# Attention outputs weighed after the products, and three of its operands turned by VectorE and DMA in place of TensorE

## The chip, the cores and the metric

The kernel runs on one core of a Trainium2 chip. A core has TensorE (PE in the profile, its weight loads PEld), VectorE (DVE), ScalarE (ACT), GpSimd (POOL) and SyncE (SP), which here only issues transfers (its issues stand as SPq). Each engine works through its own queue in order. TensorE writes to PSUM, the other engines read and write SBUF, and DMA moves data between SBUF and DRAM. The metric is the device time of one execution in microseconds (us). Before the change it is 2302.33 us, the median of 3 runs (2301.53 to 2303.08).

## The reference

The input is x, 2048 tokens of 1024 features, in float32. What is computed, cut to what matters:

```python
x = A_x
h  = x + A(layernorm(x), wq, wk, wv, wo, beta)   # Infini-attention
h2 = h + B(layernorm(h), w1, b1, w2, b2)         # layernorm, MLP 1024 -> 3584 -> 1024 with gelu

# A: 32 heads of 32 features, 4 segments of 512 tokens, one after the other
for s in range(4):
    logits = qs @ ks.T * Dh**-0.5 + mask         # per head, within the segment; causal
    a_dot  = softmax(logits) @ vs
    a_mem  = (phi(qs) @ M) / (phi(qs) @ z + 1e-6)   # phi(t) = t + 1 where t > 0, else exp(t)
    outs.append(g * a_mem + (1 - g) * a_dot)     # g = sigmoid(beta), one per head
    M += phi(ks).T @ vs                          # a 32x32 memory per head
    z += phi(ks).sum()                           # over the segment's tokens
A = concat(outs) @ wo
```

## The kernel before, in words

All products are made in float32r from two parts, a high part (the value rounded) and a low part (what is left), as three matmuls: high by high, high by low, low by high.

The program works in two halves of 1024 tokens, that is two segments each. A half has its attention first, then the product with wo, then the MLP's first layer; the MLP's second layer follows once, at the end, for all tokens.

The attention of a half is 16 **units**: 8 groups `g` of four heads, and for each the half's two segments. With segments numbered `s` = 0 to 3, the first half holds s = 0 and 1, the second s = 2 and 3, so each s has 8 units, and there are 32 in all. Queries, keys and values come out of the projections with features in the partitions (4 heads of 32) and 512 tokens along the row.

`dense` (L402) does a unit's projections: 8 steps each for keys, queries and values (`project`, L355; three matmuls of 512 columns a step). Around them it makes high and low parts (kh, kl, qh, ql) and `stack` (L372) puts these together for each head by DMA: a unit has 24 such transfers of 64 KB, all issued by SP on line 377. It also makes phi of keys (pk) and queries (pq). Three operands must be turned, so that tokens and features change places, and TensorE does it by matmuls with an identity, four of 128x128 each time:

- phi(keys), where s < 3: L453 into `pkn` in PSUM; ACT takes the high part (pkh, L455), DVE the low (pkl, L457),
- values, in every unit: ACT copies them to SBUF (vt, L461), TensorE turns them (vn, L469), ACT and DVE make the two parts of vs (L471, L472),
- what was read from the memory, where s > 0: `om` is turned on L516 into `pom`, and ACT copies that to `omt` (L521).

The memory's own small products (pm, pmm) wait in a list, and `one_small` (L383) puts one of them before a transpose or a product of the softmax part.

The softmax part of a unit runs while the next unit is projected: `heads` yields steps (L631), and `interleave` takes one for each step of `dense`. A **slot** is one head, and the string `PLAN` (L31) says what each of a slot's six steps does: `q` products of queries and keys, then mask, maximum and exponential with sums (`qk`, `soft`); `n` the weighing (`norm`, L552: DVE inverts the sums two blocks at a time, and POOL multiplies the exponentials, `pr`, by the inverse and by 1 - g, L557); `t` transposes of the weighed blocks (`ptr`, L560) with a copy to the high part; `s` the low part; `a` the products with vs (`av`, L582); `o` the output (`av_out`, L600). Three heads are under way at once: the current one (q, n), the one before (t, s) and the one before that (a, o). After a unit's fourth head POOL adds omt to the output tile ot (L607), and ot goes to DRAM.

The order on each engine is made when the program is built: the instructions are placed in the order of the program where what they need is there in time by the builder's own estimate, and a later one may be put first. PSUM has three banks for projections and turned operands (`ps_dense`); SBUF has five tiles of name `tmp`, six of `tmpr`, one `ot`.

Of the kernel before, what the change touches and what calls it, by code (L numbers as in the profile page):

```python
# [17 lines left out]
P = 128  # L18
# [12 lines left out]
PLAN = ('q1 S2', 'q0 n0 a0', 'q2 t0 a1', 'q3 n2 s0 o', 't1', 's1 t2')  # L31
# [8 lines left out]
def raw(ap):  # L40
    return ap.bitcast(F32)


def build(tc, x, wq, wk, wv, wo, beta, w1, b1, w2, b2, out):
# [8 lines left out]

    ident = const.tile([P, P], F32, name="ident")
# [29 lines left out]

    acts = {}
# [258 lines left out]
    def attention(half, first):  # L344
# [6 lines left out]

        def tmpr(name):
            return ab.tile([P, 512], F32R, tag="tmpr", name=name, bufs=6)
# [48 lines left out]
        def dense(g, sl, ws, u):  # L402
            s = 2 * half + sl
            behind = acts.pop("late", iter(()))
            kps = ws.pop("kps", None)
            if kps is None:
                kps = ps_dense("kps")
                for c in project(ws["k"], sl, "kps", kps):
                    if c >= 2:
                        next(behind, None)  # L410
                    yield
            kh, kl = tmpr("kh"), tmpr("kl")
            nc.scalar.copy(kh, kps)
            nc.vector.tensor_tensor(kl, kps, raw(kh), op=ALU.subtract)
            if s < 3:
                kparts = phi_parts(kps)
            qps = ps_dense("qps")
            for c in project(ws["q"], sl, "qps", qps):
                if c == 0:
                    u["ks"] = stack(kh, kl, "ks", (0, 1, 0))  # L420
                if c == 2 and s < 3:
                    zc = ab.tile([P, 64], F32, name="zc", bufs=2)[:, 0:1]
                    pk = phi_sum(kparts, "pk", zc)
                next(behind, None)
                yield
            qh, ql = tmpr("qh"), tmpr("ql")
            nc.scalar.copy(qh, qps)
            nc.vector.tensor_tensor(ql, qps, raw(qh), op=ALU.subtract)
            if s > 0:
                qparts = phi_parts(qps)  # L430

            vps = ps_dense("vps")
            for c in project(ws["v"], sl, "vps", vps):
                if c == 0:
                    u["qs"] = stack(qh, ql, "qs", (0, 0, 1))
                if s > 0:
                    if c == 2:
                        pq = phi_sum(qparts, "pq")
                    if c == 4:
                        while small:  # L440
                            one_small()
                        pqh, pql = tmpr("pqh"), tmpr("pql")
                        mzh = ab.tile([P, 256], F32R, name="mzh", bufs=1)[:, 0:132]
                        mzl = ab.tile([P, 256], F32R, name="mzl", bufs=1)[:, 0:132]
                        nc.scalar.copy(pqh, pq)
                        nc.gpsimd.tensor_copy(mzh, MZ[:, g, :])
                        nc.gpsimd.tensor_tensor(mzl, MZ[:, g, :], raw(mzh), op=ALU.subtract)
                    if c == 5:
                        nc.gpsimd.tensor_tensor(pql, pq, raw(pqh), op=ALU.subtract)
                if c == 1 and s < 3:  # L450
                    pkn = ps_dense("pkn")
                    for i in range(4):
                        nc.tensor.transpose(pkn[:, i * P:(i + 1) * P], pk[:, i * P:(i + 1) * P], ident)  # L453
                    pkh, pkl = tmpr("pkh"), tmpr("pkl")
                    nc.scalar.copy(pkh, pkn)  # L455
                if c == 2 and s < 3:
                    nc.vector.tensor_tensor(pkl, pkn, raw(pkh), op=ALU.subtract)  # L457
# [986 lines left out]
```

## Time and profile before

| | |
|---|---|
| time, median of 3 runs | 2302.33 us (2301.53 to 2303.08) |
| span of the profiled execution | 2296.2 us |
| busy: PE, PEld | 2270.4 us (99%), 1890.8 us (82%) |
| busy: DVE, ACT, POOL | 1540.3 us (67%), 1225.0 us (53%), 1092.4 us (48%) |
| attention of the first half, of the second | from the start to about 500 us; from about 900 to 1400 us |

The span reaches from the first instruction's start to the last one's end; the run's time holds it and what lies around it. A row of a group of instructions reads: line, engine, operation, out<-in, shapes, count, then busy time, mean ns of one, and the idle time of the engine before them with what ended it. Matmuls overlap in the pipeline, so a row's duration of one matmul is longer than the distance to the next one's start; the chain of waits counts by such distances.

### The profile page before, as it was taken

To read this page: it belongs to the slowest core of one execution; us is meant where nothing else is said; L and a number is where in the kernel's file an instruction comes from. 1 tells how busy PE (TensorE), PEld (TensorE's weight loads), DVE (VectorE), ACT (ScalarE), POOL (GpSimd) and SP (SyncE) were. 2 spreads that over 40 slices of the span, in tenths; PEclk is the share of its full clock that TensorE was granted. 3 is DMA by queue.
4 is the path that set the end of the run, shared out by engine and by line. 5 is a ranking of instruction groups with operands and counts; after the bars stand their busy time and mean duration, and the time that the engine had idled before them with its cause. 6 is when DMAs were issued, how large, how long until landed. Compare 5 with 4: busy or idle time off the path is not lost.

```text
span 2296.2 us, 35279 instructions
## 1 busy us (share of the span) xinstructions
PE 2270.4 (99%) x11769; PEld 1890.8 (82%) x11769; DVE 1540.3 (67%) x3173; ACT 1225.0 (53%) x2549; POOL 1092.4 (48%) x1134
## 2 busy tenths in 40 slices
PE   8999999999999999999999999999999999999999
PEld 6888888878888888888888887888888888888887
DVE  6777777776655565777777777565566766577563
ACT  6777777775453445777777776363344223322221
POOL 5545555555244442555555556253445554155430
PEclk9999999999999999999999999999999999999999
DMA  6333333345465654433333344466667976476762
GB/s 190 92 85 91 93 89 85 87 120 182 139 204 172 188 165 142 113 91 86 85 87 88 87 111 140 156 211 175 176 188 263 345 243 216 159 253 221 249 234 90
DMA packets 322719, 355.36 MB, mean 155 GB/s; under 512 B 26190, under 2 KB 218730, under 8 KB 322538
## 3 DMA queue, kind: packets, MB, share of 16 engines
q1 hardware_dynamic: 259370, 316.40, 45.4%
q10 hardware_dynamic: 63168, 36.71, 5.3%
q8 instruction: 93, 1.52, 0.3%
q14 instruction: 88, 0.72, 0.1%
HBM read 226.59 MB, written 76.09 MB: 132 GB/s over the span
## 4 chain that ended last, share of the span: by engine, by line
PE 91%; ACT 3%; POOL 2%; DVE 2%; issue 1%; DMA 1%; ACTq 0%; SPq 0%; POOLq 0%; DVEq 0%
PE po L1278 22%; PE bps L882 9%; PE cps L882 7%; PE dps L882 6%; PE po L593 6%; PE ppt L573 6%; PE pqk L541 3%; PE vps L116 2%; PE vps L115 2%; PE kps L115 2%; PE kps L116 2%; PE vps L117 2%; PE kps L117 2%; PE pwo L117 2%; PE pwo L116 2%; PE pwo L115 2%
## 5 line engine op out<-in xcount | busy, mean ns | idle before, releaser
L557 POOL TENSOR_SCALAR pr<-pr,nm,gate 128x128 f32<-128x128 f32 (+3 forms) x512 | 322.6, 639 | 345.9 <-DVE nm L554 260.0
L550 ACT ACTIVATE pr<-pr,mx 128x256 f32<-128x256 f32 (+3 forms) x512 | 287.6, 562 | 161.9 <-DVE mx L542 158.2
L580 DVE TENSOR_TENSOR ptl<-ppt,pth 128x512 fp32r<-128x512 f32 (+1 forms) x384 | 227.2, 599 | 86.2 <-ACT pth L575 82.0
L542 DVE CUSTOM_DVE_ANT_0 pr<-pqk,mask 128x256 f32<-128x256 f32 (+3 forms) x512 | 243.3, 484 | 46.5 <-PE pqk L541 43.7
L573 PE MATMUL ppt<-ident,pr 128*128 128x128 f32 x1280 | 223.6, 277 | 2.1 <-POOL pr L557 1.4
L575 ACT CAST pth<-ppt 128x512 fp32r<-128x512 f32 (+1 forms) x384 | 194.2, 517 | 39.0 <-PE ppt L573 33.1
L1288 DVE TENSOR_TENSOR c<-c,po 128x512 f32<-128x512 f32 x160 | 105.4, 683 | 143.1 <-PE po L1278 135.5
L573 PEld LDWEIGHTS ppt<-ident,pr 128*128 128x128 f32 x1280 | 164.6, 140 | 32.5 <-POOL pr L557 2.6
L541 PE MATMUL pqk<-ks,qs 96*128 96x256 f32 (+3 forms) x512 | 161.3, 315 | 0.0
L92 POOL TENSOR_TENSOR wl<-wr,wh 128x1024 fp32r<-128x1024 f32 x52 | 124.5, 2393 | 70.8 <-PE pqk L541 27.6
L593 PE MATMUL po<-pth,vs 128*64 128x512 f32 (+3 forms) x512 | 155.4, 326 | 0.3 <-ACT pth L575 0.2
L593 PE MATMUL po<-ptl,vs 128*64 128x512 f32 (+3 forms) x512 | 153.9, 310 | 1.3 <-DVE ptl L580 1.2
L1278 PE MATMUL po<-w2h,zh 128*128 128x512 f32 x378 | 121.1, 390 | 0.8 <-DVE zh L1218 0.4
L1135 POOL TENSOR_TENSOR w2r<-w2r 128x512 f32<-128x512 f32 x54 | 85.4, 1593 | 72.0 <-DVE c L1288 36.9
L541 PEld LDWEIGHTS pqk<-ks,qs 96*128 96x128 f32 x512 | 96.2, 188 | 21.5
L994 POOL TENSOR_TENSOR s<-r 128x512 f32<-128x512 f32 x28 | 43.6, 1559 | 143.4 <-DVE sa L1010 87.1
L882 PE MATMUL bps<-zh,sb 128*128 128x512 f32 x336 | 111.0, 391 | 0.0
L882 PE MATMUL bps<-zh,sa 128*128 128x512 f32 x336 | 110.8, 390 | 0.0
L115 PE MATMUL vps<-yh,wh 128*128 128x512 f32 x256 | 109.4, 427 | 0.9 <-DVE MZ L497 0.9
L115 PE MATMUL kps<-yh,wh 128*128 128x512 f32 (+1 forms) x264 | 110.1, 417 | 0.0
L115 PE MATMUL qps<-yh,wh 128*128 128x512 f32 x256 | 106.8, 417 | 0.0
L1278 PE MATMUL po<-w2h,hl 128*128 128x512 f32 x322 | 103.2, 390 | 0.5 <-POOL hl L1218 0.3
(241 smaller groups left out, 6657.1 us busy)
## 6 DMA issues: line engine op xcount, KB each, us to landing
hr<-h_dram SPq DMA_DIRECT2D x112, 448.0 KB, 5.4
w2r<-in_B_w SPq DMA_DIRECT2D x122, 256.0 KB, 4.4
r<-in_B_w SPq DMA_DIRECT2D x56, 512.0 KB, 4.5
h_dram<-ht ACTq DMA_DIRECT2D x84, 256.0 KB, 3.7
ks<-kh SPq DMA_DIRECT2D x256, 64.0 KB, 2.0
qs<-qh SPq DMA_DIRECT2D x256, 64.0 KB, 2.0
wr<-in_A_wo SPq DMA_DIRECT2D x32, 512.0 KB, 4.0
wx<-in_B_w SPq DMA_DIRECT2D x56, 256.0 KB, 3.5
```

Source lines behind the costliest of these rows:

```text
L115: nc.tensor.matmul(ps, ah, bh, start=first, stop=False)
L116: nc.tensor.matmul(ps, ah, bl, start=False, stop=False)
L541: nc.tensor.matmul(pqk[:, :n], u["qs"][j][:, i * P:(i + 1) * P], u["ks"][j][:, 0:n], start=True, stop=True)
L542: nc.vector.tensor_tensor_reduce(out=st["pr"][:, offs[i]:offs[i] + n], in0=pqk[:, :n], in1=mask[:, 512 - n:512], op0=ALU.add, op1=ALU.min, ...
L550: nc.scalar.activation(pi, pi, AF.Exp, bias=mx[:, i:i + 1], scale=-1.0, accum_out=mx[:, 4 + i:5 + i])
L557: nc.gpsimd.tensor_scalar(pi, pi, nm[:, 4 + k:5 + k], gate[:, 1, 4 * g + j:4 * g + j + 1], op0=ALU.mult, op1=ALU.mult)
L573: nc.tensor.transpose(ppt[:, o:o + P], pr[:, offs[i] + jk * P:offs[i] + (jk + 1) * P], ident)
L575: acts["pth"] = n, nc.scalar.copy(pth[:, base:base + w], ppt[:, :w])
L580: nc.vector.tensor_tensor(o, x0, x1, op=ALU.subtract)
L593: nc.tensor.matmul(po[:, P * jk:], v, st[part][:, koff[jk]:koff[jk] + w], start=(jk, part) == (0, "pth"), stop=(jk, part) == (2, "ptl"))
L882: nc.tensor.matmul(ps, x_[:, c, :], y_[:, c, :], start=first and c == 0 and n == 0, stop=last and c == 3 and n == 2, skip_group_check=True)
L1278: nc.tensor.matmul(ps, x_[:, k], y_[k], start=opens and k == 0 and i == 0, stop=closes and k == self.KP - 1 and i == 2, skip_group_check=True)
```

## The change

Three things change in the attention; the MLP and the product with wo stay.

1. *The weighing.* `norm` goes: the exponentials are turned and multiplied with vs as they are. `inverse` (`r` in PLAN) makes the inverse of a head's four sums, and, at the fourth head, multiplies them by 1 - g on POOL. `weigh` (`w`), once in a unit, turns these 16 columns by one TensorE transpose, copies them to SBUF, stores them in DRAM and loads them back spread over the partitions, as a tile w of 128x512. `av_out` multiplies the unit's output by w on POOL.
2. *The turning.* `turned` takes the place of the TensorE transposes of values, phi(keys) and om: DVE transposes within 32x32 blocks, SP stores the result in DRAM (256 KB) and loads it back in four transfers of 32 partitions, which puts the blocks in their places. The tiles for it are taken from the pool of the half (`zt`), whose tiles wo_first uses afterwards. The heads' and blocks' order in vs changes with it, and POOL makes pkl.
3. *The order.* `dense` becomes a table: `TIMES` gives each part a step, 0 to 23 in the unit's own projections, 24 and more in the next unit's. PLAN is new as well. The parts for `VT`, `KT` or `OT` being False are not used.

```diff
-PLAN = ('q1 S2', 'q0 n0 a0', 'q2 t0 a1', 'q3 n2 s0 o', 't1', 's1 t2')
+VT, KT, OT = True, True, True
+TIMES = dict(pk=10, kx=15, pkh=21, pkl=22, ks=12, qs=16, pq=17, pqh=19, pql=20, omt=20, vx=23, pm=25, vs=32, vl=33, pmm=38, om=37, omc=40)
+PLAN = ('r', 'q0', 'a0 S2 t0 q2 s0', 'a1 q1 o', 't1 s1 w q3', 't2')
...
+    PKL, VSL, GTE = nc.gpsimd, nc.vector, nc.gpsimd
...
+    turn_dram = [dram.tile([P, 512], F32, name=f"turn_dram{k}") for k in range(6)]
+    r_dram = [dram.tile([16, P], F32, name=f"r_dram{k}") for k in range(2)]
...
+        scr = [acts["zt"].tile([P, 4, 512], F32, tag=f"t{x_}3", name=f"sc{x_}") for x_ in "hl"]
+
+        def turned(src, to, mid):
+
+            nc.vector.transpose(mid.rearrange("p (c k d) -> p c k d", c=4, k=4), src.rearrange("p (k c d) -> p c k d", c=4, k=4))
+            d = turn_dram[acts.get("turned", 0) % len(turn_dram)]
+            acts["turned"] = acts.get("turned", 0) + 1
+            nc.sync.dma_start(d, mid)
+            for c in range(4):
+                nc.sync.dma_start(to[32 * c:32 * c + 32].rearrange("j (h x) -> j h x", h=4),
+                                  d[:, c * P:(c + 1) * P].rearrange("(h j) x -> j h x", h=4))
...
+            def on(name, fn):
+                t = T[name]
+                (todo if t < 24 else after).setdefault(t % 24, []).append(fn)
...
+            def key_turn():
+                v["kn"] = scr[1][:, 2 + sl]
+                turned(v["pk"], v["kn"], scr[1][:, 0])
+
+            def key_halves():
+                v["pkh"], v["pkl"] = tmpr("pkh"), tmpr("pkl")
+                v["pkn"] = v["kn"].rearrange("p (h k d) -> p k h d", h=4, k=4)
+                v["pk4"] = [x_.rearrange("p (k h d) -> p k h d", h=4, k=4) for x_ in (v["pkh"], v["pkl"])]
+                nc.scalar.copy(v["pk4"][0], v["pkn"])
+
+            def key_lower():
+                PKL.tensor_tensor(v["pk4"][1], v["pkn"], raw(v["pk4"][0]), op=ALU.subtract)
...
+            def value_turn():
+                v["vn"] = scr[0][:, 2 + sl]
+                turned(ps["v"], v["vn"], scr[0][:, 0])
...
+            def value_halves():
+                v["vn3"] = v["vn"].rearrange("p (h k e) -> p h k e", h=4, k=4)
+                nc.scalar.copy(vs.rearrange("p (h k) e -> p h k e", h=4)[:, :, :, 0:32], v["vn3"])
+
+            def value_lower():
+                v4 = vs.rearrange("p (h k) e -> p h k e", h=4)
+                VSL.tensor_tensor(v4[:, :, :, 32:64], v["vn3"], raw(v4[:, :, :, 0:32]), op=ALU.subtract)
...
+            def memory_turn():
+                while v.get("read") != 1:
+                    one_small()
+                turned(v["om"], u["omt"], tmp("omx"))
...
-        def norm(st, i):
-            pr, mx, nm, j, g = st["pr"], st["mx"], st["nm"], st["j"], st["u"]["g"]
-            nc.vector.reciprocal(nm[:, 4 + i:6 + i], mx[:, 4 + i:6 + i])
-            for k in (i, i + 1):
-                pi = pr[:, offs[k]:offs[k] + P * (k + 1)]
-                nc.gpsimd.tensor_scalar(pi, pi, nm[:, 4 + k:5 + k], gate[:, 1, 4 * g + j:4 * g + j + 1],
-                                        op0=ALU.mult, op1=ALU.mult)
+        def inverse(st):
+            u, j = st["u"], st["j"]
+            if j == 0:
+                u["rs"] = ab.tile([P, P], F32, name="rs", bufs=1)
+            rs = u["rs"]
+            nc.vector.reciprocal(rs[:, 4 * j:4 * j + 4], st["mx"][:, 4:8])
+            if j == 3:
+                r4 = rs[:, 0:16].rearrange("p (h i) -> p h i", i=4)
+                GTE.tensor_tensor(r4, r4, gate[:, 1, 4 * u["g"]:4 * u["g"] + 4].unsqueeze(2).to_broadcast([P, 4, 4]),
+                                        op=ALU.mult)
+
+        def weigh(st):
+            u, j = st["u"], st["j"]
+            if j < 3:
+                return
+            n = acts["weighed"] = 1 - acts.get("weighed", 0)
+            w = u["w"] = tmp("w") if u["g"] == NG - 1 and u["s"] % 2 else scr[n][:, 1]
+            pw = ps_dense("pw")
+            nc.tensor.transpose(pw[0:16, 0:P], u["rs"][:, 0:16], ident)
+            nc.scalar.copy(w[0:16, 0:P], pw[0:16, 0:P])
+            d = r_dram[n]
+            nc.sync.dma_start(d, w[0:16, 0:P])
+            nc.sync.dma_start(w, bass.AP(tensor=d.tensor, offset=d.offset, ap=[[512, 4], [0, DH], [1, 512]]))
...
-                v = u["vs"][:, 4 * jk + j, :]
+                v = u["vs"][:, 4 * j + jk, :]
...
             if j == 3:
+                nc.gpsimd.tensor_tensor(ot, ot, u["w"], op=ALU.mult)
                 if u["omt"] is not None:
-                    nc.gpsimd.tensor_tensor(ot, ot, u["omt"], op=ALU.add)
+                    if OT:
+                        ot4 = ot.rearrange("p (k c j) -> p k c j", k=4, c=4)
+                        nc.gpsimd.tensor_tensor(ot4, ot4, u["omt"].rearrange("p (c k j) -> p k c j", k=4, c=4), op=ALU.add)
```

More of the change, by code (lines that the diff above doesn't have):

```diff
@@ L427, in dense @@
[L427 to L435, printed above, removed]
-                if s > 0:
[L437 to L457, printed above, removed]
-                next(behind, None)
-                yield
@@ L530, in attention @@
+            run(24)
+            acts["carry"] = after
         offs = [0, 128, 384, 768]
```

245 lines of the change are left out of this document (153 added, 92 removed).

## The prediction

> **What bounds the kernel now.** I read the page's busy line and chain first, then the windows of the two attention stretches, since nothing else is changed.
>
> ```profile
> span 2296.2 us, 35279 instructions
> PE 2270.4 (99%) x11769; PEld 1890.8 (82%) x11769; DVE 1540.3 (67%) x3173; ACT 1225.0 (53%) x2549; POOL 1092.4 (48%) x1134
> PE 91%; ACT 3%; POOL 2%; DVE 2%; issue 1%; DMA 1%; ACTq 0%; SPq 0%; POOLq 0%; DVEq 0%
> ```
> ```profile
> 100.00:300.00 200.00, 199.60 (x1220) 169.31 (x1219) 148.50 (x437) 145.45 (x370) 105.38 (x148) 1.00 0.33 83
> 1000.00:1200.00 200.00, 200.00 (x1225) 169.69 (x1224) 151.59 (x452) 146.81 (x373) 112.51 (x150) 1.00 0.35 88
> ```
>
> A window's row gives its length, then PE, PEld, DVE, ACT and POOL busy, the granted clock (1.00), the DMA engines' busy share and GB/s. In both stretches PE is busy all the time, DVE three quarters, ACT nearly as much, POOL a half, the DMA engines a third. A busy PE could still hide waits, so I looked at who makes PE wait, in the waits, and at the chain through a middle stretch (its row: start, us, what).
>
> ```profile
> PEld po L593 <- DVE ptl L580: 8.5, 19, 0.7
> PEld pmm L395 <- ACT r L364: 2.1, 7, 0.3
> PE ppt L573 <- POOL pr L557: 1.4, 4, 0.5
> POOL pr L557 <- DVE nm L554: 260.0, 120, 9.8
> ```
> ```profile
> 181.88 0.44 PE pkn L453 x4
> 192.63 0.44 PE vn L469 x4
> 199.05 0.59 ACT kh L413
> ...
> 260.94 0.59 ACT kh L413
> ```
>
> POOL's weighing makes PE wait 1.4 us in all; its own 260 us are waits of an engine that nobody waits for. So PE's stream of matmuls is the bound in the attention, and its time there is the sum of the distances between its starts. The copies of keys to kh are one per unit; two units lie between 199.05 and 260.94 (a third copy between them is not on the chain), which makes 30.95 us a unit and, at 24 steps, 1.29 us a step.
>
> **Part 1: what leaves TensorE.** The rows of the three turned tiles give the counts.
>
> ```profile
> L469 PE MATMUL vn<-ident,vt x128: 271/272/329, 40.6 to 1380.8; 128*128 128x128 f32 x128
> L453 PE MATMUL pkn<-ident,pk x96: 270/272/273, 31.5 to 1333.3; 128*128 128x128 f32 x96
> L516 PE MATMUL pom<-ident,om x96: 270/296/331, 80.5 to 1387.9; 128*128 128x128 f32 x96
> ```
>
> These are 128 + 96 + 96 = 320 transposes, 80 groups of four. Which price: the duration of one is 272 ns, but the chain puts a group of four at 0.44 us, 110 ns each, what it takes to start the next work. For pkn and vn that row is the very thing. The four of pom have small products between them:
>
> ```profile
> 204.26 0.22 PE L395 MATMUL pmm<-vs,pkl 128*128 128x128 f32 x1
> 204.32 0.27 PE L516 MATMUL pom<-ident,om 128*128 128x128 f32 x1
> 204.35 0.31 PE L395 MATMUL pmm<-vs,pkh 128*128 128x128 f32 x1
> 204.50 0.30 PE L516 MATMUL pom<-ident,om 128*128 128x128 f32 x1
> ```
>
> From small product to transpose 0.06 us, then 0.03, then 0.15: a pair takes 0.18 to 0.19, so a transpose adds up to 0.13 us, a group 0.5 us. But the small products are not removed; they go between other transposes or products and pay part of it there. I take 0.44 for all: 80 x 0.44 = 35.2 us, upper end 38. The unknown is only whether the time stays gone.
>
> [...]
>
> **Part 2: what comes to TensorE.** `weigh` makes one transpose in each of 32 units. A quarter of a group is 0.11 us, and alone it is no more than a group's 0.44: 3.5 to 14 us. I take 3.5, since the group's 0.44 is nearly even per transpose.
>
> **Part 3: the other engines, which must not become late.**
>
> ```profile
> L472 DVE TENSOR_TENSOR vs<-vn,vs 128x512 fp32r<-128x512 f32 x32 | 22.0, 686 | 0.7 <-ACT vs L471 0.4 <-DMA qs<-qh 0.3
> L457 DVE TENSOR_TENSOR pkl<-pkn,pkh 128x512 fp32r<-128x512 f32 x24 | 16.3, 680 | 1.1 <-ACT pkh L455 1.1
> L369 DVE SCALAR_TENSOR_TENSOR pk<-e,r 128x512 f32<-128x512 f32 x24 | 21.5, 894 | 20.4 <-ACT r L364 20.4
> L686 DVE CAST oh<-orr 128x512 fp32r<-128x512 f32 x8 | 3.3, 416 | 0.0
> L554 DVE RECIPROCAL nm<-mx 128x2 f32<-128x2 f32 x256 | 42.0, 164 | 86.2 <-ACT pr L550 85.6
> L557 POOL TENSOR_SCALAR pr<-pr,nm,gate 128x128 f32<-128x128 f32 (+3 forms) x512 | 322.6, 639 | 345.9 <-DVE nm L554 260.0 <-PE qps L117 37.2 <-PE vps L117 13.2
> L607 POOL TENSOR_TENSOR ot<-ot,omt 128x512 f32<-128x512 f32 x24 | 30.9, 1287 | 27.4 <-DVE ot L604 27.4
> L461 ACT COPY vt<-vps 128x512 f32<-128x512 f32 x32 | 18.9, 592 | 1.0 <-PE vps L117 0.9
> L521 ACT COPY omt<-pom 128x512 f32<-128x512 f32 x24 | 14.2, 590 | 0.3
> ```
>
> DVE: 80 block transposes of 128x512. No row shows one; the nearest whole-tile rows are 416 ns (a copy from SBUF) and 894 ns (two inputs). I take the 686 ns of one pass over a PSUM tile: 55 us, between 33 and 72. The lower part of vs now reads two SBUF operands, 686 to 894 ns, 7 us more. Gone: 128 of 256 inversions (21 us) and pkl (16 us). Net +25 us, -4 to +42, in some 1000 us: DVE from 75% to 77%. The cover is its idle quarter.
>
> POOL: -323 us of weighing; + 32 weighings of an output, 24 lower parts of pk, and 32 small multiplications that cost at most as much: 88 x 1.29 = 114 us. A relief on an engine nobody waits for: nothing.
>
> ACT: the 32 copies to vt and 24 to omt go (33 us); 32 copies of 16x128, at most 0.59 us each (19 us), come. Nothing either way. But ACT now has two copies (pkh, the high part of vs) that wait for a DMA, and behind them in its queue stand exponentials and the copies that TensorE's next transposes and products need. This is the step that can go wrong.
>
> **Part 4: SP's queue and the way through DRAM.**
>
> ```profile
> 204.30 0.59 SPq L377 DMA_DIRECT2D ks<-kl  x1
> 204.94 0.59 SPq L377 DMA_DIRECT2D ks<-kh  x1
> 205.62 0.53 SPq L609 DMA_DIRECT2D o_dram<-ot  x1
> 212.04 0.51 SPq L377 DMA_DIRECT2D ks<-kh  x1
> ```
> ```profile
> L377 SPq DMA_DIRECT2D ks<-kh x256: 507/581/1293, 25.8 to 1364.9; - x128
> ```
> ```profile
> ks<-kh SPq DMA_DIRECT2D x256, 64.0 KB, 2.0
> o_dram<-ot SPq DMA_DIRECT2D x28, 256.0 KB, 2.3
> orr<-o_dram SPq DMA_DIRECT2D x28, 256.0 KB, 3.2
> ```
>
> SP's issue of a 64 KB transfer holds its queue 0.58 us. A unit now: 24 stacks, 13.9 us, and about 1.3 us for ot (0.53) and one and a half loads of weights, taken at the like price. After: five transfers for each turn (2.9 us), two turns in a unit of s = 0 or 3, three in one of s = 1 or 2, and two for w (1.2 us). That makes 13.9 + 1.3 + 1.2 + 5.8 = 22.2 us in half the units and 25.1 in the other 16, of a unit of about 30. It fits, if SP does not stand idle while a store lands (2.3 us from issue, 1.8 after its issue ends). SP did stand idle before, at no cost: after 205.62 it waited for a key tile until 212.04.
>
> A turn takes 0.7 (DVE) + 2.3 (store) + 3 x 0.58 + 2.0 (last load lands) = 6.7 us, 7.9 with the 3.2 of a load from DRAM. phi(keys) is turned at step 15 and wanted at 21: 6 x 1.29 = 7.7 us, just enough with nothing in front. Values: 23 to 32, 11.6 us. The read memory: step 13 of the next unit to step 9 of the one after it, 26 us. w: 2.3 + 3.2 plus copy and transpose, some 6.5 us, for five steps, 6.5 us; if late, POOL waits and ot goes out later, with a slot (7.7 us) until it is written again. The stacks of keys move from step 8 to 12 and stand in front of the phi(keys) store: nine of them take 5.2 us, four steps, so that turn can be 2 to 3 us late. Then ACT waits at pkh, or its instructions were placed in another order to begin with.
>
> DMA engines: the 2.5 turns of a unit move 1.3 MB more, on about 83 GB/s x 30.95 us = 2.6 MB; busy share from a third to a half: covered.
>
> At the end of each half the tiles of `zt` come free only when the last unit's vs and w are used (step 9 of its heads), so wo_first's fourth weight tile is late by up to 4 steps, 5 us, twice; PE has heads in between: 0 to 10, I take 2. Waits for qs, which now stands behind two turns in SP's queue: 0 to 1 us in 16 units; I take 2 in all, because PE waits nearly nowhere in a kernel that had such waits on SP before.
>
> **Sum**, against the profiled execution: span 2296.2 - 35.2 + 3.5 + 2 + 2 = 2268.5. Its run's time lies 2302.3 - 2296.2 = 6.1 us above the span (by the median of the runs): **2275 us**, 1.2% faster. Its own range is 2262 (38 us out, no waits) to 2292 (14 for w's transposes and 10 at the ends).
>
> **Rivals.**
>
> *SP becomes the bound (slower).* With each of the four landings in a unit of three turns waited out in SP's queue, that unit needs 25.1 + 4 x 1.8 = 32.3 us of SP, while TensorE needs about 30. It decides from 30 us on, that is once three of the four ((30 - 25.1) / 1.8 = 2.7) are not filled with other transfers. Price 16 x 2.3 = 37 us on the forecast: 2312, up to 2340 if also the two-turn units wait. For it: the row at 205.62, where SP idles 6 us for a tile. Against it: an order that put the ot store there while the keys' tile was not free. [...] No row here shows a VectorE transpose.
>
> *ACT waits for the turned keys (about the same).* In 24 units 3 us late at pkh; a third of it reaching TensorE, since exponentials run a slot's part ahead, is 24 us: 2299. For it the six steps of 7.7 us; against it the six steps themselves, if SP is free.
>
> *The duration is the price.* 320 x 0.272 = 87 us go instead of 35: 2223. The chain's 0.44 for four speaks against it.
>
> *The transposes were free.* Were PE's stream limited by DVE or ACT, taking matmuls away would bring nothing. Both have a quarter idle in the windows, and PE's waits are a few us: no more than 2 in 100.
>
> **Chances.** Forecast 0.52; SP 0.33; ACT 0.10; duration 0.03; free 0.02. What a measurement can tell from no change is 0.2%, 4.6 us: faster means below 2297.7, slower above 2306.9. The forecast's 0.52, the duration's 0.03 and a part of ACT's (0.03) are faster: 0.58. ACT's 0.05 and the free case's 0.02 are the same: 0.07. SP's 0.33 and ACT's last 0.02 are slower: 0.35. The range reaches from the forecast's lower end, 2262, to 2328, inside the SP case, and leaves some 2 in 10 out.
>
> **What would show it.** Right: no L453, L469, L516; PE idle as little as now; distance between kh copies near 29.9 us; DVE transposes near 0.69 us; SPq issues near 24 us a unit. Wrong: SPq waiting on its own turn stores; ACT waiting for a DMA at pkh or vs; PE waiting on pth, ptl or qs; a DVE transpose of more than 0.9 us.

## The result, and the profile after

The changed kernel takes 2372.59 us (2367.16 to 2377.42) beside 2302.07 us for the kernel before on the same chip: 1.0307 times as long, with a 95% interval of 1.029 to 1.0324. It is 3.1% slower where 1.2% faster was forecast. Its profiled execution has a span of 2368.4 us, 72.2 us more than before.

The page of the changed kernel, its row of the cores, and its windows of the same two stretches (columns as before: length, busy PE, PEld, DVE, ACT, POOL, granted clock, DMA share, GB/s):

```profile
span 2368.4 us, 34856 instructions
PE 2278.4 (96%) x11481; PEld 1872.3 (79%) x11481; DVE 1556.7 (66%) x3101; ACT 1209.7 (51%) x2525; POOL 853.8 (36%) x710
```
```profile
core 0: 2368.4 us, clock 0.988
```
```profile
100.00:300.00 200.00, 188.77 (x1091) 156.10 (x1090) 142.92 (x401) 135.42 (x345) 56.67 (x59) 0.97 0.52 136
1000.00:1200.00 200.00, 187.95 (x1093) 153.72 (x1092) 143.48 (x411) 135.16 (x346) 59.33 (x57) 0.98 0.50 134
```

PE now stands idle for 11 to 12 us of each 200, and its granted clock, 1.000 before, falls to 0.97 and 0.98. No other engine has become full: DVE, ACT and POOL are all busy for less of a stretch than before. So nothing is the bound in the sense of a sum; things come late. Whose waits they are is in the waits (engine, line, what it waited for: us in all, times, longest):

```profile
PE po L709 <- DVE ptl L696: 16.9, 16, 2.7
PE pwo L121 <- POOL zl L97: 11.5, 4, 4.3
PE po L709 <- DVE ot L720: 8.8, 7, 3.0
PE pqk L641 <- DMA qs<-ql: 6.9, 7, 1.6
ACT ot L714 <- DMA o_dram<-ot: 39.3, 20, 5.8
DVE wh L94 <- DMA wr<-in_A_wv: 19.0, 7, 3.5
POOL ot L722 <- DMA scl<-r_dram: 28.7, 5, 9.7
SPq L730 <- POOL ot L726: 104.7, 21, 5.7
SPq L730 <- POOL ot L722: 26.2, 7, 4.3
SPq L366 <- DMA turn_dram<-sch: 21.5, 29, 2.0
```

SyncE's queue (SPq) waits 131 us at L730, the store of a unit's output ot, for GpSimd's sum; whatever stands behind that store waits too: from 216.32 to 220.33 us it issues nothing, the store goes out when GpSimd's product with w ends (220.30), and the next stack at 220.73. One late weight block shows what comes of a late queue. The timeline (start, us, what, in brackets the idle time before and its releaser), SyncE first, then VectorE, then PE:

```profile
203.15 0.53 SPq L364 DMA_DIRECT2D turn_dram<-sch  x1
203.72 0.46 SPq L331 DMA_DIRECT2D wr<-in_A_wv  x1
```
```profile
208.20 0.70 DVE L94 CAST wh<-wr 128x1024 fp32r<-128x1024 f32 x1 [3.41 <-DMA wr<-in_A_wv]
209.82 1.01 DVE L696 TENSOR_TENSOR ptl<-ppt,pth 128x512 fp32r<-128x512 f32 x2
```
```profile
208.23 0.34 PE L709 MATMUL po<-pth,vs 128*64 128x384 f32 x1
210.56 0.43 PE L709 MATMUL po<-ptl,vs 128*64 128x384 f32 x1 [2.00 <-DVE ptl L696]
```
```profile
206.00:210.00 4.00, 2.56 (x12) 1.64 (x11) 1.80 (x6) 0.54 (x2) 0.97 (x1) 1.00 1.11 272
211.00:214.00 3.00, 3.00 (x13) 2.61 (x13) 2.12 (x8) 2.75 (x7) 0.69 (x2) 0.50 0.29 67
215.00:219.00 4.00, 4.00 (x25) 3.33 (x23) 3.94 (x13) 2.43 (x8) 0.00 (x0) 1.00 0.46 127
```

The weights' load went out at 203.72, behind the stacks of queries and a turn's store. VectorE stands 3.41 us at the cast of that block, in order; the lower half ptl, behind it, is late (its high part was ready at 205.12, by ScalarE's cast on L691); PE waits 2.00 us; and then PE runs at half its clock (the last three rows are windows: 0.50 from 211 to 214): the 128x512 products for qps at 211.97, 212.39 and 212.82 start 0.42 to 0.43 us apart, those at 215.54, 215.78 and 216.00 0.22 to 0.24. Thirteen such stretches, of 3.41 or 6.83 us, 58 us in all, stand in this trace, and a last one where the span ends, as before the change. The mean clock of 0.988 over the span is worth 0.012 x 2368.4 = 28 us, an estimate.

**Where the 72 us are.** The copies of keys to kh, one a unit, sixteen a half, split the span. Before, then after (the last two numbers ahead of the shapes are the first and last start):

```profile
L413 ACT CAST kh<-kps x16: 563/566/587, 25.2 to 480.2; 128x512 fp32r<-128x512 f32 x16
L413 ACT CAST kh<-kps x16: 563/587/590, 900.1 to 1351.9; 128x512 fp32r<-128x512 f32 x16
```
```profile
L439 ACT CAST kh<-kps x16: 562/586/591, 25.6 to 501.1; 128x512 fp32r<-128x512 f32 x16
L439 ACT CAST kh<-kps x16: 564/586/590, 934.5 to 1410.6; 128x512 fp32r<-128x512 f32 x16
```

The units of the first half take 475.5 instead of 455.0 us, those of the second 476.1 instead of 451.8: +44.8 us. The way from the sixteenth copy to the seventeenth, the first half's end, takes 433.4 instead of 419.9, and from the last copy to the span's end 957.8 instead of 944.3: +27 us. The rest is the start.

### The profile page after: what moved, and what is told of

Its sections match the earlier page's. It is cut to its first block, busy times and chain, and to the rows that moved or that the text cites. A ratio compares the mean times of both kernels' runs of the same rounds, so it can differ in the third digit from the quotient of the medians.

```text
span 2368.4 us, 34856 instructions
## 1 busy us (share of the span) xinstructions
PE 2278.4 (96%) x11481; PEld 1872.3 (79%) x11481; DVE 1556.7 (66%) x3101; ACT 1209.7 (51%) x2525; POOL 853.8 (36%) x710
## 5 line engine op out<-in xcount | busy, mean ns | idle before, releaser
L650 ACT ACTIVATE pr<-pr,mx 128x128 f32<-128x128 f32 (+3 forms) x512 | 288.6, 564 | 164.0 <-DVE mx L642 155.0
L642 DVE CUSTOM_DVE_ANT_0 pr<-pqk,mask 128x128 f32<-128x128 f32 (+3 forms) x512 | 246.1, 482 | 99.4 <-PE pqk L641 97.1
L691 ACT CAST pth<-ppt 128x512 fp32r<-128x512 f32 (+1 forms) x384 | 195.2, 512 | 75.6 <-PE ppt L689 69.9
L641 PE MATMUL pqk<-ks,qs 96*128 96x128 f32 (+3 forms) x512 | 184.8, 362 | 13.9 <-DMA qs<-ql 6.9
L720 DVE TENSOR_TENSOR ot<-po,ot 32x512 f32<-32x512 f32 x128 | 87.1, 681 | 56.6 <-ACT ot L714 55.0
L709 PEld LDWEIGHTS po<-ptl,vs 128*64 128x64 f32 x512 | 69.0, 137 | 48.4 <-DVE ptl L696 25.6
L122 PE MATMUL qps<-yh,wl 128*128 128x512 f32 x256 | 102.9, 402 | 2.8 <-POOL wl L97 2.8
```

Of the source, the lines that this page charges most:

```text
L641: nc.tensor.matmul(pqk[:, :n], u["qs"][j][:, i * P:(i + 1) * P], u["ks"][j][:, 0:n], start=True, stop=True)
L642: nc.vector.tensor_tensor_reduce(out=st["pr"][:, offs[i]:offs[i] + n], in0=pqk[:, :n], in1=mask[:, 512 - n:512], op0=ALU.add, op1=ALU.min, ...
L650: nc.scalar.activation(pi, pi, AF.Exp, bias=mx[:, i:i + 1], scale=-1.0, accum_out=mx[:, 4 + i:5 + i])
L691: acts["pth"] = n, nc.scalar.copy(pth[:, base:base + w], ppt[:, :w])
L709: nc.tensor.matmul(po[:, P * jk:], v, st[part][:, koff[jk]:koff[jk] + w], start=(jk, part) == (0, "pth"), stop=(jk, part) == (2, "ptl"))
```

## The experiments

All comparisons are with the kernel before, run on the same chip. The builder places instructions anew with each edit, so an edit also moves what stands near it; single differences under some 10 us are read with that in mind. The same rows of kh give this table for the kernels on which the reading rests (us of one profiled execution, whose span can stand some 5 us off the median time: the fifteen units of a half, and what follows them to the next half or the end):

| kernel | units 1 | end 1 | units 2 | end 2 | time | ratio, 95% interval |
|---|---|---|---|---|---|---|
| before | 455.0 | 419.9 | 451.8 | 944.3 | 2302 | 1 |
| table alone (e6) | 456.1 | 420.1 | 462.5 | 948.3 | 2312.76 | 1.0041 [1.0026, 1.0056] |
| table, weighing (e2) | 452.5 | 431.0 | 459.2 | 953.9 | 2327.99 | 1.0112 [1.0097, 1.0128] |
| table, turns, old PLAN (e7) | 462.8 | 423.6 | 468.9 | 947.8 | 2333.55 | 1.0135 [1.0114, 1.0156] |
| the change | 475.5 | 433.4 | 476.1 | 957.8 | 2372.59 | 1.0307 [1.029, 1.0324] |
| no DMAs of turns (e9) | 436.0 | 434.2 | 436.4 | 960.5 | 2294.35 | 0.9969 [0.9959, 0.9978] |
| DMAs of turns unwatched (e10) | 476.7 | 437.4 | 478.7 | 955.4 | 2378.72 | 1.0336 [1.0318, 1.0354] |
| the same by GpSimd (e17) | 457.8 | 434.3 | 467.1 | 955.9 | 2347.43 | 1.0201 [1.0184, 1.0218] |
| the change, ot's store by GpSimd (e12) | 457.7 | 428.0 | 470.6 | 955.5 | 2340.23 | 1.017 [1.0155, 1.0185] |

### The parts of the change alone

**e2, weighing alone.**

```diff
-VT, KT, OT = True, True, True
+VT, KT, OT = False, False, False
```

> Edit: VT, KT and OT False: the three operands are turned on TensorE again, by the branches that the changed kernel has for it; the weighing by w and the new table of steps stay. Theory 'SP's queue is too full with the turns': the waits of DVE for weights and of ACT for turned tiles go, the clock stays at 1.00, and TensorE has its 35 us of transposes back: about 2302 + 4 = 2306, at most 2320 with w's waits. Theory 'w holds ot': ACT's waits for the ot store stay, 2325 to 2345. Theory 'the new order is the fault': 2340 or more, with waits that no DMA ends.

Measured 2327.99 us. The time lies in the range of 'w holds ot', but the place does not fit that theory: the units lose little (2.5 us shorter, 7.4 longer), the half ends lose 11.1 + 9.6 us.

**e6, the table alone.** As e2, and besides the old PLAN with `norm`, without `inverse`, `weigh` and the product with w:

```diff
-PLAN = ('r', 'q0', 'a0 S2 t0 q2 s0', 'a1 q1 o', 't1 s1 w q3', 't2')
+PLAN = ('q1 S2', 'q0 n0 a0', 'q2 t0 a1', 'q3 n2 s0 o', 't1', 's1 t2')
...
-                nc.gpsimd.tensor_tensor(ot, ot, u["w"], op=ALU.mult)
```

> The table of places alone: no turn, the exponentials normalised by GpSimd in the old order of the heads' steps, values, phi(keys) and retrieved values transposed by TensorE. Theory (turns and w make the loss, the places make none): 2295 to 2306 us, as before. Rival (the new places themselves cost, since copies and sums now stand at other steps of the in-order queues): over 2312 us, with PE waits that the kernel before does not have.

Measured 2312.76 us: just over the rival's bound. The new places alone cost 0.4%; in the profiled execution the units of the second half are 10.7 us longer (from 905 to 1350 us PE stands idle for 7.8 us, before for 1.2). The prediction had no term for that.

**e3 and e7, the turns without w.** Both bring `norm` back in place of w. e3 keeps the new PLAN's order, e7 takes the old one.

```diff
+PLAN = ('', 'q0', 'a0 S2 t0 q2 s0', 'a1 q1 n0 o', 't1 s1 q3', 't2 n2')    # e3
+PLAN = ('q1 S2', 'q0 n0 a0', 'q2 t0 a1', 'q3 n2 s0 o', 't1', 's1 t2')     # e7
```

> Edit: the exponentials are weighed as in the kernel before (inverse by DVE, multiplication by POOL, n0 and n2 put in steps 3 and 5 of a slot), and w goes; the turns through DRAM and the table stay. Theory 'SP's queue is too full with the turns': DVE still waits 3 us for a weight block in every second unit and the clock still halves behind it, 2340 to 2370. Theory 'w holds ot': 2270 to 2300, since the turns alone take 35 us from TensorE and nothing else is late.

> The three turns by VectorE and DMA with the table, but the heads' steps in the old order and the exponentials normalised by GpSimd as before, no w. PE is spared all the 44 groups of four transposes at 0.44 us. Theory (the way through DRAM is late for the in-order ACT and SyncE is too full for the weights): slower than before, 2310 to 2355 us, with the waits for weight blocks and for turned tiles of the changed kernel. Rival (w and the held ot tile are the cause, the turns are not): 2270 to 2290 us.

e3 measured 2367.75 us, ratio 1.0288 [1.0272, 1.0303], and tells little, though the first theory's range held: I had put `norm` so late that PE waits for GpSimd's weighed exponentials.

```profile
PE ppt L698 <- POOL pr L658: 60.9, 99, 3.2
```

e7, without that, measured 2333.55 us: the turns cost 21 us on top of the table alone, although TensorE is spared 80 groups of transposes (the 44 of the expectation is a slip). The theory's range held. With 9 to 11 us for the table, 15 for weighing and 21 for turning, 45 to 47 of the 70 us are explained by the parts; together they cost some 24 us more than one by one.

### What it is about the turns

**e9, the DVE transposes without their DMAs.**

```diff
-            nc.vector.transpose(mid.rearrange(...), src.rearrange(...))
-            ... the store, the four loads
+            nc.vector.transpose(to.rearrange(...), src.rearrange(...))
```

> The changed kernel with the DVE transposes but without their way through DRAM: the DVE transpose writes the turned tile itself, the store and the four loads of every turn are left out (so values, phi(keys) and retrieved values are turned only inside blocks of 32). PE is spared the same transposes, w is as in the change. Theory (the turns lose by their DMAs alone): 2285 to 2305 us, that is the table alone (2313) less 24 us of PE stream and plus 6 to 15 us for w. Rival (DVE's transposes, w and the order of the steps lose by themselves): over 2330 us.

**e10, the DMAs issued, and nobody waiting for them.**

```diff
+            nc.vector.transpose(to.rearrange(...), src.rearrange(...))
-            nc.sync.dma_start(d, mid)
+            nc.sync.dma_start(d, to)
-                nc.sync.dma_start(to[32 * c:32 * c + 32].rearrange("j (h x) -> j h x", h=4),
+                nc.sync.dma_start(mid[32 * c:32 * c + 32].rearrange("j (h x) -> j h x", h=4),
```

> As the run without the way through DRAM, but the store and the four loads of every turn are issued by SyncE at their places; the loads land in the scratch tile that nobody reads (what is computed from the turns is again turned only inside blocks of 32). It has the load on SyncE's queue and on the DMA engines and no wait of ScalarE for a turned tile. Theory A (SyncE's full queue makes weights and output stores late): most of the loss stays, 2340 to 2375 us. Theory B (ScalarE and GpSimd wait in order for turned tiles): most of it goes, 2285 to 2310 us.

e9 measured 2294.35 us, e10 2378.72 us. e9 is where its theory had it, e10 4 us above theory A's range. Without the DMAs 78 us go; with them issued and their data unused, all of it is there again. So no consumer's wait for a turned tile is needed for the loss.

**e4, the turns' DMAs issued by GpSimd** (watched as in the change):

```diff
-            nc.sync.dma_start(d, mid)
+            nc.gpsimd.dma_start(d, mid)
-                nc.sync.dma_start(to[32 * c:32 * c + 32]...
+                nc.gpsimd.dma_start(to[32 * c:32 * c + 32]...
```

> Edit: the turns' stores and loads are issued from POOL's queue, the rest as after. Theory 'SP's queue is too full with the turns': SP has its 17 us a unit again, the waits of DVE for weights go; POOL stands at its own stores but has two thirds of its time free: 2290 to 2330. Theory 'w holds ot': the load of w is no faster, 2345 to 2372, or worse, since POOL makes ot too and now waits for stores to land.

Measured 2449.65 us, ratio 1.0645 [1.0629, 1.0661], far from the first theory. Now the turned tiles are late, and ScalarE waits for them in order, for 163 us where the change has 20:

```profile
ACT vs L522 <- DMA sch<-turn_dram: 111.2, 30, 8.5
ACT pkh L459 <- DMA scl<-turn_dram: 51.7, 14, 8.0
```

**e13, as e10, with loads that wait for no store,** and **e17, as e13, with store and loads issued by GpSimd.**

```diff
-                                  d[:, c * P:(c + 1) * P].rearrange("(h j) x -> j h x", h=4))
+                                  x[0, 0:P, c * P:(c + 1) * P].rearrange("(h j) x -> j h x", h=4))   # e13, e17
-            nc.sync.dma_start(
+            nc.gpsimd.dma_start(     # e17, at all five
```

> As the run with the unwatched turns (2379 us), but the four loads of every turn read the input x instead of what the turn has stored, so SyncE never waits for a turn's store to land; number, size and places of the DMAs are the same (nobody uses what they bring, and values, phi(keys) and retrieved values are turned only inside blocks of 32). Theory A (SyncE's issue time alone): within 8 us of it, 2370 to 2387 us. Theory B (SyncE's in-order wait for the landing of each turn's store, some 2 us three times a unit): 25 to 50 us less, 2330 to 2355 us.

> As the run whose turns' loads wait for no store (2390 us; turned only inside blocks of 32), but the turns' stores and loads are issued by GpSimd's queue. The bytes and the DMAs stay, SyncE is left with the work that it had without the turns (16.3 us a unit), GpSimd gets some 8 us of issue a unit on top of 36% busy. Theory A (SyncE's queue is the cause): 2294 to 2330 us. Theory B (the bytes on the DMA engines, or a chip-wide lateness of DMAs): 2360 us or more.

e13 measured 2389.68 us, ratio 1.0384 [1.0369, 1.04], no less than e10: SyncE's wait for its own stores to land is not the cause. e17 measured 2347.43 us, between the two theories. The window of 200 to 470 us, in the order e9, e10, e13, e17:

```profile
200.00:470.00 270.00, 270.00 (x1619) 226.74 (x1618) 218.00 (x592) 201.84 (x512) 82.59 (x84) 1.00 0.37 99
```
```profile
200.00:470.00 270.00, 257.82 (x1513) 212.55 (x1511) 199.64 (x553) 186.35 (x475) 79.05 (x80) 0.99 0.54 141
```
```profile
200.00:470.00 270.00, 252.99 (x1478) 208.38 (x1479) 199.77 (x538) 183.19 (x465) 80.91 (x80) 0.99 0.50 132
```
```profile
200.00:470.00 270.00, 269.61 (x1620) 226.18 (x1619) 218.71 (x597) 200.74 (x510) 110.68 (x131) 1.00 0.46 127
```

In the same 270 us PE gets through 1619 matmuls without the DMAs, 1513 and 1478 with them in SyncE's queue, and 1620 in e17. That looks as if the bytes cost nothing and SyncE's queue all, but this window does not show it. The loads of e13 and e17 wait for nothing, and in e17 the builder placed most of them in the first four units of each half. Of their loads, e17 has 20 in this window (first row), e13 91:

```profile
L366 POOL DMA_DIRECT2D omx<-in_A_x x20: 548/562/611, 220.4 to 464.1; - x20
```
```profile
L366 SPq DMA_DIRECT2D scl<-in_A_x x39: 312/430/1753, 204.9 to 469.6; - x39
L366 SPq DMA_DIRECT2D sch<-in_A_x x36: 323/430/609, 207.0 to 468.2; - x36
L366 SPq DMA_DIRECT2D omx<-in_A_x x16: 394/426/446, 225.7 to 421.4; - x16
```

The stores are there in both (23 and 21), so half of the turns' bytes, issued by GpSimd, cost nothing that shows here. The loads' bytes are not tested in this window. e17 loses 21.8 us against e9 in the first half's units and 30.7 in the second's, and nearly all of it (20.1 and 26.6 us) in the first four units of each, where the loads are. GpSimd is busy there for 106 of 129 us and for 100 of 135 (its issues count as busy), where e9 has 38 of 109 and 35 of 108:

```profile
27.80:156.50 128.70, 114.98 (x646) 94.00 (x645) 86.78 (x230) 81.76 (x200) 106.40 (x172) 0.96 0.70 185
919.90:1054.60 134.70, 119.11 (x649) 96.88 (x649) 88.46 (x233) 78.66 (x194) 99.76 (x156) 0.94 0.65 174
```

The DMA engines are busier there too (0.70 and 0.65 by these rows, where e9 has 0.38 from 100 to 470 us and from 950 to 1320), and no run tells which of the two costs the 47 us. What e17 shows is that the same number and size of DMAs, out of SyncE's queue and at other places, cost 42 us less than in e13.

One issue is short beside its transfer here (0.43 to 0.59 us of SyncE, where a transfer of keys landed in 2.0 us before), but the issues of a unit add up to 22 us of its 32.

### What in SyncE's queue

**e12, ot's store issued by GpSimd,** and **e14, the same in e10.**

```diff
-                    nc.sync.dma_start(o_dram[u["s"]][u["g"]], ot)
+                    nc.gpsimd.dma_start(o_dram[u["s"]][u["g"]], ot)
```

> The changed kernel, with the store of ot issued by GpSimd's queue, right behind the sum that it needs, instead of SyncE's, where it waits for that sum with the stacks of the next units behind it. Theory (the blocked SyncE makes stacks, weights and turns of the second half late): SyncE's waits at L730 (131 us in 28) go, and 10 to 25 us of time, 2347 to 2362 us. Rival (ot is held by w's load, not by the queue): within 6 us of the changed kernel, 2366 to 2378 us.

> As the run with the unwatched turns (2379 us; turned only inside blocks of 32), but the store of ot is issued by GpSimd. Theory (SyncE's wait in order for ot's sum, with stacks and weights behind it, is the largest part): 30 to 60 us less, 2320 to 2350 us. Rival (issue time and landings hold it): less than 20 us less, over 2359 us.

e12 measured 2340.23 us, 32 us less than the change and better than the range given. The bytes are the same here, so these 32 us are those of SyncE's queue and not of the bytes. The store that waits in order is the largest single part that I found. ScalarE still waits for ot (69.5 us in e12), so ot's own lateness is not what the 32 us were; that leaves the work behind the store. e14 measured 2365.32 us, ratio 1.0278 [1.0261, 1.0295], only 13 us less than e10, on the rival's side. So the store is not all of it.

**e18 and e16, ot's store by GpSimd in e7.**

> Turns with the table and the old order of the heads' steps, the exponentials normalised by GpSimd, no w (2334 us), and the store of ot issued by GpSimd. If the store of ot holds SyncE here too: 2305 to 2325 us. If only w makes ot late (w's landing was what GpSimd's sum waited for) and without w the store waits little: 2328 to 2340 us. Below 2295 us it would beat the kernel before; that is not expected, since the table alone costs 9 us and the turns' DMAs more than PE is spared.

> Turns with the table and the old order of the heads' steps, the exponentials normalised by GpSimd, no w (2334 us).

e18 measured 2335.1 us, ratio 1.0141 [1.0121, 1.0162], the same as e7. The range of 'only w makes ot late' held, its reason only in part: in e7 (last row below) SyncE stands at ot's store too, and moving the store brings nothing. In e9 (first two rows) it stands there for 73 us, and its units are the shortest of the table. So a wait at this store is not a cost by itself; it cost 32 us in the change, 13 in e10 and nothing in e7.

```profile
SPq L724 <- POOL ot L720: 56.0, 21, 3.7
SPq L724 <- POOL ot L716: 16.9, 7, 3.2
```
```profile
SPq L738 <- POOL ot L734: 54.5, 21, 5.7
```

e16 was by mistake the kernel of e7 again, and gave 2333.98 us beside its 2333.55.

**e1, w loaded by four DMAs instead of one.**

```diff
-            nc.sync.dma_start(w, bass.AP(tensor=d.tensor, offset=d.offset, ap=[[512, 4], [0, DH], [1, 512]]))
+            for k in range(4):
+                nc.sync.dma_start(w[32 * k:32 * k + 32], bass.AP(tensor=d.tensor, offset=d.offset + 512 * k, ap=[[0, DH], [1, 512]]))
```

> Edit: the tile w is loaded by four transfers of 32 partitions in place of one whose outermost dimension is 4. In the changed kernel POOL's weighing of ot starts 5.3 to 5.7 us after that load is issued in nearly every unit. Theory 'w holds ot' (the late load keeps POOL, then ot's store, then SP and ACT's next copy into ot waiting): the distance falls to 2 to 3 us, ACT's 39 us of waits for o_dram<-ot nearly go, and 15 to 25 us of the 70 come back, about 2350. Theory 'SP's queue is too full with the turns': three more issues a unit, 2372 to 2385, with the waits for the ot store gone and those for weights and turned keys the same or longer.

Measured 2463.12 us, ratio 1.0708 [1.0688, 1.0728]: 90 us more for three more issues a unit, and far outside both ranges. Four such issues of 0.42 us instead of one of 0.58 are 1.1 us of SyncE's time a unit, 35 us in all units at the most, so the issue time alone can't be 90 us. The new entries also moved the weights' loads in the queue. That the order in the queue, and what then waits for it, makes the rest is likely and not shown.

**e11, the weights cast by GpSimd,** so VectorE has nothing that waits for a weight block:

```diff
-                ws[n] = load_block(wp, w, g * P, 3, "vector" if g or n == "k" else "scalar",
+                ws[n] = load_block(wp, w, g * P, 3, "gpsimd" if g else "vector" if n == "k" else "scalar",
```

> The changed kernel, with the upper halves of the weight blocks cast by GpSimd instead of VectorE, so VectorE has no instruction that waits for a weight block. Theory (VectorE's in-order wait for a late weight block makes ptl late, PE waits some 2 us and the clock halves): PE's waits for ptl and the half-clock stretches of the first half go, 10 to 20 us less, 2352 to 2362 us. Rival (the lateness only moves, since the blocks land as late as before): 2366 us or more, with PE waiting for GpSimd's wl or for another tile.

Measured 2365.62 us, ratio 1.0282 [1.0263, 1.0302], a little below the rival's 2366: the wait moved to GpSimd's cast, and PE waits as long for ptl (22.7 us in 25 waits, 21.9 in 21 in the change). The chain at 203 to 214 us is a symptom: in e10, which loses as much, VectorE waits for weight blocks only 4.2 us in the first half's units, where the change has 19.9. In e9, with the cast on VectorE, there is no such wait there.

### The half ends

**e5, the last units off the zt tiles; e8, the same for weighing alone; e15, e5 and e12 together.**

```diff
-            w = u["w"] = tmp("w") if u["g"] == NG - 1 and u["s"] % 2 else scr[n][:, 1]
+            w = u["w"] = tmp("w") if u["g"] == NG - 1 else scr[n][:, 1]
...
-            if VT:
+            if VT and not (g == NG - 1 and sl == 1):
                 on("vx", value_turn)
```

> The changed kernel, but the last unit of each half no longer uses the zt tiles (its values are transposed by TensorE again, its weights w and those of the unit before it stand in a tmp tile). Theory (the half ends lose because the output projection's fourth weight tile waits for the zt tiles): both half ends come back from +13.5 us to near +3 us each, the wait of L121's matmul on GpSimd's zl goes, and the time falls by 18 to 27 us, to 2346 to 2355 us. Rival (the half ends only inherit lateness from the units ahead of them): less than 6 us less, 2366 to 2373 us.

> Weighing of the outputs alone (no turn), with w of the last two units of a half in a tmp tile instead of a zt tile. Theory (most of what weighing alone lost, 26 us, was at the half ends and from the zt tile): 2303 to 2312 us, some 16 to 24 us less than with weighing alone. Rival (w's way through DRAM holds ot in all units, and the half ends only add it up): 2322 us or more.

> The changed kernel with both mends: ot's store issued by GpSimd, and the last units of a half off the zt tiles. If the two add up: 2340 less 4 to 15 us, 2325 to 2337 us. If the freed queue makes the zt tiles the next to be late, more: down to 2318 us. If they don't add: 2338 to 2345 us.

e5 measured 2369.04 us, ratio 1.0284 [1.0261, 1.0307], 3.6 us less than the change: the rival. The wait for zl fell from 11.5 to 5.9 us, and others came (oh, wh, ht at the same place), so the first half's end still takes 433.1 us. e8 measured 2318.8 us, ratio 1.0068 [1.0048, 1.0087], 9 us less than e2, between the two. e15 measured 2351.07 us, ratio 1.0213 [1.0198, 1.0228], 11 us *more* than e12 alone; the mends do not add. What holds the half ends is not the zt tile in the main. It comes with w: the table alone has +0.2 and +4.0 us there, turns with the old PLAN +3.7 and +3.5, weighing +11.1 and +9.6. Some 6 us of e8's first end are waits for the later weight halves of wo that the table alone has only 2 us of:

```profile
PE pwo L121 <- POOL wl L97: 1.9, 1, 1.9
PE pwo L121 <- POOL zl L97: 1.8, 1, 1.8
PE pwo L120 <- ACT wh L96: 1.5, 1, 1.5
PE pwo L121 <- DVE wl L97: 0.8, 1, 0.8
```

Why weighing makes those halves late was not found. No run that computes the whole result beats the kernel before; e9, the only one below it, leaves the turns' second half out.

## Why the prediction was wrong

**Part 1, what leaves TensorE, was right.** e9 differs from e2 only by the turns without DMAs (and the copies and lower parts that go with them): units of 436.0 and 436.4 us instead of 452.5 and 459.2, so 39.3 us. Of the 80 groups 74 lie between these copies, 37 in each half. In the first half, where PE of e2 is always busy, that is 16.5 us, 0.45 us a group; the term took 0.44. In the second it is 22.8 us, but there e2's PE stands idle for 6.7 us by the second row:

```profile
30.00:480.00 450.00, 450.00 (x2742) 380.18 (x2741) 324.51 (x921) 332.29 (x840) 111.59 (x122) 1.00 0.38 100
905.00:1350.00 445.00, 438.35 (x2649) 368.49 (x2648) 319.38 (x909) 322.47 (x811) 127.80 (x131) 1.00 0.38 100
```

Over the whole run e9 is some 33 us below e2, beside the term's 35.2. Neither the row's duration (87 us) nor "free" was near.

**Part 2 was not seen alone.** Weighing in place of `norm`, with its PLAN, makes the units 6.9 us shorter (e2 against e6), w's transposes included.

**Part 3, the other engines, was right in its sizes.** A block transpose takes 0.705 us (0.69 was taken):

```profile
L361 DVE STREAM_TRANSPOSE sch<-vps x32: 705/705/717, 38.6 to 1434.9; 128x512 f32<-128x512 f32 x32
L366 SPq DMA_DIRECT2D sch<-turn_dram x128: 303/425/1500, 47.2 to 1446.0; - x128
L674 SPq DMA_DIRECT2D sch<-r_dram x14: 579/584/592, 114.8 to 1413.9; - x14
L722 POOL TENSOR_TENSOR ot<-ot,sch x14: 1275/1289/1463, 120.1 to 1419.5; 128x512 f32<-128x512 f32 x14
```

It named "two copies that wait for a DMA" as the step that can go wrong. In the change ScalarE waits there for turned tiles only 20 us in all, and e10 shows the loss without them. In e4 they are 163 us.

**Part 4 is the step that failed: "It fits, if SP does not stand idle while a store lands".** The sum fitted: SyncE's issues take 22.3 us a unit, added up from the trace between the copies of keys (the short first unit of a half left out), where 22.2 to 25.1 were predicted (a turn's load takes 0.425 us, not 0.58), of units of 32.5 us; it was 15.0 before. The conclusion did not follow. Ten free microseconds a unit were no cover, because SyncE's queue, in order, spent them where it happened to wait (131 us at ot's store), and what stood behind went out late. The stacks of queries show it. Counted off in the traces, as medians over the last eleven units of each half, the first of them goes out 0.6 us after the copy to qh in e9, 4.4 in e13 and 4.6 in the change, while it lands 2.1 us after its issue in all three. The third, the last that a unit's first product needs, has left the queue 6.3 us ahead of that product in the kernel before, 8.4 in e9, 3.9 in e13 and 1.9 in the change. This lead is not the whole either: in e14 it is back at 6.4 us, and e14 is still 2.8% slower than the kernel before. Before, SyncE was ahead, and waited at the stacks (L377 then, L394 now) for tiles to come free, with 16 free microseconds a unit. The waits of the queue before, and the longest at the stacks after:

```profile
SPq L377 <- ACT pr L550: 221.2, 39, 10.9
SPq L377 <- PE pqk L541: 112.2, 38, 5.8
```
```profile
SPq L394 <- ACT kh L439: 24.8, 12, 3.1
```

In the sum "2 to 3 us late" was priced at nothing, and so was the wait of ot's store. The turns' DMAs cost 79.2 us in the units (the change against e9).

**The rival "SP becomes the bound" had the place right, not the mechanism.** It charged the landings of SyncE's own stores; e13 shows that taking the loads' wait for them away saves nothing. Its 2312, up to 2340, was too small, and so the range ended at 2328. (Its other end, 2262, is a span: the 6.1 us up to the time were not added.) In the units ot's store is 23 of the 79 us (e12). What makes up the rest, another delay of SyncE's or the DMA engines, stays open, and so does how far it depends on the order in the queue, as e1 suggests. The DVE transposes by themselves were not the cost: e9 has them and takes 2294.35 us.

**Also in Part 4:** GpSimd uses w 5.3 to 5.6 us after its load is issued (the last two rows above, first and last of 14; 5.3 is the least of all 32), where 3.2 was taken; that makes GpSimd's sum, and so ot's store, late (GpSimd waits 54.6 us for w in 12 waits). The half ends were put at 2 us (0 to 10) and cost 27, of which weighing alone has 20.7; the named cause, the zt tiles, is a small part. This term failed too. In e9, with no DMA of a turn, the units are 34.4 us shorter than before and the half ends 30.5 us longer, so only 0.3% of the forecast's 1.2% is left even then.

**Not in the prediction at all:** the table's own 9 to 11 us, and the clock: the PE wait of 2.00 us at 210.56 was followed by 3.41 us at half clock, worth some 1.7 us more by an estimate, half of that stretch.

## What to carry to other kernels

SyncE's queue, which issues in order, was not covered here by its share of free time (some 10 of 32.5 us a unit); how far it ran ahead said more (the third stack of queries was out 6.3 us ahead of its product before, 1.9 in the change). Ask for each entry what it waits for, and which entries behind it are due while it waits. To price work moved onto DMAs, run it once with the DMAs issued and nobody waiting (e10, 2378.72 us beside e9's 2294.35); a second run that issues them from another queue separates the queue from the bytes only if the DMAs keep their places, so count them in the window that is read (20 loads in e17, 91 in e13). PE was full here, and its waits were not cheap: look at the granted clock after each (0.50 for 3.41 us after the one at 210.56).

## What the runs showed of the hardware

In the change a PE wait of 2.00 us is followed by 3.41 us at half clock, in the rows at 210.56 and 211 to 214. The length of the wait does not decide it alone. The first wait below is longer, and the clock stays at 1.00 from 341 to 344 us; the second is shorter, and the clock is 0.50 from 1392 to 1395:

```profile
340.95 0.39 PE L709 MATMUL po<-ptl,vs 128*64 128x384 f32 x1 [2.23 <-DVE ptl L696]
1390.55 0.44 PE L709 MATMUL po<-pth,vs 128*64 128x512 f32 x1 [1.84 <-DVE ot L720]
```

In this trace the half-clock stretches start whole multiples of 3.4133 us apart: the three behind the waits that end at 210.56, 275.29 and 1316.04 start at 210.77, 275.63 and 1316.69, which is 19 and then 305 such lengths. What decides whether a wait is followed by such a stretch was not shown, and no run was made for it. A higher clock was not time by itself: e5's mean clock is 0.993 instead of 0.988, worth 12 us by the same estimate as above (0.005 x 2368.4), and its time is 3.6 us less, while other waits grew (PE's for qs from ql, 10.1 us instead of 6.9).
